# An adaptive-norm transformer block on one core: attention's channels in chunks of 112, score edges folded by 32, and an engine order written out

## The chip, the cores and the metric

The kernel runs on one core of one Trainium2 chip. The metric is the device time of one execution in microseconds, as the median of several runs. The core's engines work side by side, each through its own instructions in order: PE (matrix products), DVE (vector), ACT (activation functions), POOL (general), and SP, which here only issues DMAs. They wait for each other by semaphores.

## The reference

One sequence of 2048 positions with 448 channels goes through windowed attention and then a gated MLP that also mixes positions. Both halves are modulated by a vector c. Cut to what matters:

```python
mod = (silu(c) @ w_mod).reshape(1, 6, 1, 448)         # sa, ca, ga, sb, cb, gb
h = layernorm(x) * (1 + ca) + sa
q, k, v = heads(h @ wqkv)                             # 16 heads of 28
s = where(0 <= i - j < 256, q @ k.T * 28 ** -0.5, -1e9)
x = x + ga * (softmax(s) @ v) @ wo
h = layernorm(x) * (1 + cb) + sb
z = gelu(h @ w_in)                                    # 448 -> 1792
z1, z2 = z[..., :896], layernorm(z[..., 896:])
x = x + gb * ((z1 * (w_sp @ z2 + b_sp)) @ w_out)      # w_sp: 2048 x 2048
```

A query sees itself and the 255 positions before it. In blocks of 128 positions these lie in three key blocks: its own (lower triangle), the one before (all of it) and the one before that (upper triangle).

## The kernel before

Positions are 16 tiles of 128 in four blocks of 512. The 448 channels are the contraction of every projection and are held transposed (`hT`, channels on partitions) as four chunks: three of 128 and one of 64. The fourth chunk's other 64 rows are zeroed once in each weight (`t_p2`, `t_p3`, `t_p3v`, `t_p4`, lines 491 to 494), and products run over all 128 rows.

**Start.** `load3` (line 418) loads the columns of w_mod for the first modulation and then those of w_q and w_k together, each in three pieces over the queues of ACT and SP. The first four tiles of x come ahead of them in two pieces, one per queue. `t_mA` makes the modulation's columns, `mod_out` copies them to `modT`, and each chunk of the transposed, normalised x is scaled and shifted on its way out of PSUM into `hT` (lines 691 and 693). `t_wqk` (lines 595 and 596) copies the weights into `WQK`, where each head has 32 columns instead of 28. `warm` puts pairs of identity matmuls on PE as fillers; they have the lowest priority.

**Attention.** For each tile j, Q and K are projected into `qT` and `KT` (lines 725, 760 and 785; four heads in a group, 32 partitions a head) and V into `Vaug` (798). The scores are made with keys on partitions, in two halves of two head groups each (`half`; `qs` names the groups). In `fm` (line 901), four matmuls, one per head of a group, run on four row tiles of 32 partitions of the PE array, each into a PSUM bank of its own. In each bank of 512 columns stand: the middle key block for the first group (128 columns), and 192 columns for each group with the two triangles. Of both triangles a 64 x 64 corner is never seen, and two corners share 64 columns on different partitions: these products take 64 keys each, on column tiles of 64. The middle block of the second group has no room in the banks. It comes from one product of `KT` with `QBD`, a copy of Q in which each head's 32 partitions stand in columns of their own with zeros elsewhere, so that a single 512-column product gives four heads (line 910). `QBD` is filled by four DMAs a block (751, 777) into zeros that ACT wrote (`t_qz`, 528).

`unit` adds a product and the exp that empties it (line 862): per half one of 4 x 512 columns into `PW`, then one of 512 columns from the `QBD` product. `mask_all` (917) multiplies both triangles by 0/1 masks and spreads them out into `PT`, once per head group. The products with V (944) follow per head group; a column of ones in `Vaug` gives the row sums. Lines 958 and 960 divide. SP transposes the result by DMA into `hT`, `wo_g` projects it (969), 973 adds the residual, and statistics (603 to 609, with a power operation on POOL), normalisation (616, 622, 626), a DMA transpose and the second modulation (994) make the MLP's input.

**MLP.** Line 1066 makes z2 and 1087 z1, with two row tiles of 64 partitions; 1110 is the product with w_sp, and 1127 the last projection.

**What sets the order.** Each operation is added to a `Sched` with its dependences, a priority, PSUM banks or buffers that it takes (`Hold`, `Res`) and a duration on every engine that may run it: evictions from PSUM may run on ACT or DVE, some modulations on POOL too. `Sched.order` is a list planner. It keeps a clock per engine and takes, engine by engine, the operation that can start first, by priority among those; so it chooses engine, order and buffer. `PACE`, `PSTEP` and `LEAD` tie the next blocks' projections to the scores. `count` and `waits` turn the order into semaphore counts, and `emit` writes each engine's instructions.

Of the kernel before, what the change touches and what calls it, by code (L numbers as in the profile page):

```python
# [4 lines left out]
ACT = mybir.ActivationFunctionType  # L5
BF16 = mybir.dt.bfloat16
F32 = mybir.dt.float32

ENGS = ("pe", "act", "dve", "pool", "sp")
HOP = 0.12  # L10

BIAS = 0.0

NEXT = {"dve": 0.08, "act": 0.11, "pool": 0.045}

SHAPE = 0.1

TURN = 1.1
# [11 lines left out]
class Res:  # L30
# [6 lines left out]

    def best(self):
        found = None
        for o in self.options:  # L40
            at = 0.0
            for u in o:
                h = self.last[u]
                if h is None:
                    continue
                if not h.until or any(x.end is None for x in h.until):
                    at = None
                    break
                at = max([at] + [x.end for x in h.until])
            if at is not None and (found is None or at < found[0]):  # L50
                found = (at, o)
        return found
# [10 lines left out]
class Op:  # L63
    def __init__(self, n, ways, deps, prio, take, table, dma, lat, tail):
# [17 lines left out]
        self.shape = "full"  # L82

# [4 lines left out]
class Sched:  # L88
# [23 lines left out]
    def order(self):  # L112
        ready = {e: [] for e in ENGS}
        for op in self.ops:
            op.left = len(op.deps)
            for d in op.deps:
                d.users.append(op)
        free = {e: 0.0 for e in ENGS}
        table = [None]
        turned = [True]  # L120
        shape = ["full"]
        self.prog = {e: [] for e in ENGS}
        dma_at = [0.0]

        def enter(op):
            op.ready = max([0.0] + [d.start + d.ways["pe"][0] if d.eng == "pe" and "pe" in op.ways else d.end for d in op.deps])
            for e in op.ways:
                ready[e].append(op)

        for op in self.ops:  # L130
            if not op.left:
                enter(op)
        todo = len(self.ops)
        while todo:
            pick = None
            for e in ENGS:
                found = []
                for op in ready[e]:
                    if any(x.start is None for x in op.after):
                        continue  # L140
                    at = max(op.ready, free[e])
                    ok = True
                    for h in op.take:
                        b = h.res.best()
                        if b is None:
                            ok = False
                            break
                        at = max(at, b[0])
                    if ok:
                        found.append((at + (BIAS if e == "act" and len(op.ways) > 1 else 0.0), op))  # L150
                if not found:
                    continue
                first = max(free[e], min(a for a, _ in found))
                at, op = min(((a, o) for a, o in found if a <= first + 1e-9), key=lambda x: (x[1].prio, x[1].n))
                if pick is None or at < pick[0]:
                    pick = (at, e, op)
            assert pick is not None, "no op can go on"
            at, e, op = pick
            if e == "act" and len(op.ways) > 1:
                at -= BIAS  # L160
            for h in op.take:
                _, slot = h.res.best()
                h.slot = slot
                for u in slot:
                    old = h.res.last[u]
                    if old is not None:
                        op.deps.update(old.until)
                    h.res.last[u] = h
            op.deps.discard(op)
            dur, fns = op.ways[e]  # L170
            if e == "act" and op.table and op.table != table[0]:
                dur += 1.3
            if e == "pe" and op.shape != shape[0]:
                dur += SHAPE
                shape[0] = op.shape
            if e == "sp":
                if op.turn and not turned[0]:
                    dur += TURN
                turned[0] = op.turn
            op.eng, op.start = e, at  # L180
            free[e] = at + dur - NEXT.get(e, 0.0)
            if op.land is not None:
                op.end = max(at + 1.0, op.land)
                dma_at[0] = max(dma_at[0], op.end - 2.0)
            elif op.dma:
                dma_at[0] = max(dma_at[0], at + 1.0) + op.lat
                op.end = dma_at[0] + op.tail
            else:
                op.end = at + dur + HOP + op.lat
            if e == "act" and op.table:  # L190
                table[0] = op.table
            for x in op.ways:
                ready[x].remove(op)
            self.prog[e].append(op)
            todo -= 1
            for u in op.users:
                u.left -= 1
                if not u.left:
                    enter(u)
# [1010 lines left out]
```

## Time and profile before

| | |
|---|---|
| runs | 289.79, 290.8 and 291.15 us; median 290.8 |
| span of the profiled execution | 288.0 us, first to last instruction |
| PE | busy 274.4 us, 3432 matmuls |
| DVE | busy 170.3 us, 365 instructions |
| ACT | busy 131.8 us, 153 instructions |
| POOL | busy 123.4 us, 192 instructions |
| granted PE clock | 1.00 throughout |
| first projection on PE | 12.97 us (its weight load) |
| score exps (L862) | from 20.5 to 118.6 us, 69.4 + 6.1 us of ACT |
| products with w_sp (L1110) | from 167.1 us |

The profiled execution's own time is not listed apart from its span; against the median of the runs 2.8 us lie around the span. The span starts with the first instruction. A matmul's duration holds its way through the array, and matmuls overlap; so PE's busy time says when it had something in flight, and its rate is read from the distance between starts. Stages are best read from the chain of work that ended last and from busy time by stretches.

### The profile page before, as it was taken

Reading aid. Unit: us, or ns where it says so; the run is one execution under the profiler, and the core shown is the slowest. Engines: PE = TensorE matmul, PEld = TensorE weight load, DVE = VectorE, ACT = ScalarE, POOL = GpSimd, SP = SyncE. Lnnn points to the kernel's source line nnn. Section 1 sums busy time; section 2 is a strip of 40 time slices with the busy share of each in tenths; the row PEclk is TensorE's granted clock in tenths of the full one; section 3 lists DMA queues with packets and bytes.
Section 4 is the critical chain, followed back from the end, with each engine's and each line's share of the span. In section 5 each row is a group of like instructions: output and inputs, shape, how many; then the busy total and the mean of one; then the engine's idle time right before and its main releaser. Section 6 shows DMA issues by size and latency. Waiting matters only on the chain.

```text
span 288.0 us, 7864 instructions
## 1 busy us (share of the span) xinstructions
PE 274.4 (95%) x3432; PEld 151.4 (53%) x3432; DVE 170.3 (59%) x365; ACT 131.8 (46%) x153; POOL 123.4 (43%) x192
## 2 busy tenths in 40 slices
PE   6798889999999999999979999999999999999997
PEld 2595557567666765544445544444444444444443
DVE  7679996988889999879998101113211231123223
ACT  4487979999999988775656720000000000000000
POOL 8041690761470749898654113333133303330331
DMA  7845936244233685320199899940100010001001
GB/s 213 267 156 148 326 60 95 54 83 92 39 41 76 112 166 58 60 58 18 39 186 167 194 175 190 186 77 17 49 0 0 2 64 0 2 0 64 0 2 64
DMA packets 65349, 25.92 MB, mean 90 GB/s; under 512 B 56417, under 2 KB 64226, under 8 KB 65314
## 3 DMA queue, kind: packets, MB, share of 16 engines
q1 hardware_dynamic: 64496, 24.26, 40.3%
q10 hardware_dynamic: 818, 1.15, 1.3%
q8 instruction: 27, 0.44, 0.7%
q14 instruction: 8, 0.07, 0.1%
HBM read 9.01 MB, written 1.84 MB: 38 GB/s over the span
## 4 chain that ended last, share of the span: by engine, by line
PE 64%; DVE 20%; POOL 5%; DMA 5%; issue 2%; SPq 2%; ACT 1%; ACTq 1%; POOLq 0%
PE ps L1110 34%; PE ps L1127 7%; PE ps L1087 5%; DVE st_all L603 5%; DVE PT L917 5%; PE ps L785 4%; DMA wq_st<-in_A_wqkv_dram 3%; PE ps L944 2%; POOL rs_all L609 2%; PE ps L798 2%; PE ps L1066 2%; PE ps L901 2%; PE ps L725 2%; DVE xn L616 1%; DVE x_sb L973 1%
## 5 line engine op out<-in xcount | busy, mean ns | idle before, releaser
L862 ACT ACTIVATE PW<-ps 128x2048 bf16<-128x2048 f32 (+1 forms) x56 | 69.4, 1239 | 4.5 <-PE ps L901 3.2
L1117 POOL TENSOR_TENSOR z1T<-tmpg,z1T 128x512 bf16<-128x512 bf16 x28 | 32.3, 1153 | 89.9 <-DVE tmpg L1114 89.9
L1114 DVE TENSOR_TENSOR tmpg<-ps,bsp_bc 128x512 bf16<-128x512 f32 x28 | 19.4, 692 | 85.3 <-PE ps L1110 85.3
L1110 PE MATMUL ps<-wspB,z 128*128 128x512 bf16 x224 | 48.8, 379 | 0.0
L1110 PE MATMUL ps<-wspA,z 128*128 128x512 bf16 x224 | 48.7, 379 | 0.0
L917 DVE TENSOR_TENSOR PT<-PW,mask 128x1024 bf16<-128x1024 bf16 x56 | 38.7, 718 | 0.7 <-ACT PW L862 0.3
L1110 PEld LDWEIGHTS ps<-wspA,z 128*128 128x128 bf16 x224 | 21.9, 98 | 26.5 <-issue 0.4
L1110 PEld LDWEIGHTS ps<-wspB,z 128*128 128x128 bf16 x224 | 21.9, 98 | 26.4
L608 POOL TENSOR_SCALAR ve_all<-mv_all 128x1 f32<-128x1 f32 (+2 forms) x37 | 10.1, 274 | 47.3 <-DVE mv_all L606 46.5
L944 PE MATMUL ps<-Vaug,PT 128*128 128x32 bf16 x496 | 26.2, 177 | 2.8 <-issue 1.7
L944 PEld LDWEIGHTS ps<-Vaug,PT 128*128 128x128 bf16 x496 | 22.9, 96 | 7.0 <-issue 1.8
L609 POOL TENSOR_TENSOR rs_all<-ve_all,neghalf 128x1 f32<-128x1 f32 (+2 forms) x37 | 24.8, 672 | 2.0
L1066 PE MATMUL ps<-w_in,hT 64*128 64x448 bf16 x224 | 22.4, 349 | 2.1 <-POOL rs_all L609 1.7
L1087 PE MATMUL ps<-hT,w_in 64*128 64x512 bf16 x196 | 21.8, 376 | 0.0
L1127 PE MATMUL ps<-w_out_g,z1T 128*128 128x448 bf16 x112 | 21.8, 352 | 0.0
L944 PE MATMUL ps<-Vaug,PW 128*128 128x32 bf16 x224 | 21.7, 176 | 0.0
L944 PEld LDWEIGHTS ps<-Vaug,PW 128*128 128x128 bf16 x224 | 17.9, 96 | 2.9
L603 DVE BATCH_NORM_STATS2 st_all<-x_sb 128x6 f32<-128x448 bf16 x32 | 18.9, 609 | 0.4 <-DMA x_sb<-in_A_x_dram 0.3
L1073 ACT ACTIVATE z<-ps 128x896 bf16<-128x896 f32 x16 | 13.9, 915 | 11.2 <-PE ps L1066 11.2
L603 DVE BATCH_NORM_STATS2 st_all<-z 128x6 f32<-128x448 bf16 x32 | 18.1, 594 | 1.0 <-ACT z L1073 1.0
L622 POOL TENSOR_SCALAR xn<-x_sb,rs_all,ve_all 128x448 bf16<-128x448 bf16 x17 | 18.1, 1066 | 0.9
L1066 PEld LDWEIGHTS ps<-w_in,hT 64*128 64x128 bf16 x224 | 11.0, 94 | 12.5 <-ACT z1T L1095 2.1
(106 smaller groups left out, 370.1 us busy)
## 6 DMA issues: line engine op xcount, KB each, us to landing
out_dram<-fin SPq DMA_DIRECT2D x16, 112.0 KB, 1.7
x_sb<-in_A_x_dram SPq DMA_DIRECT2D x3, 448.0 KB, 4.4
wmod<-in_w_mod_dram SPq DMA_DIRECT2D x1, 1344.0 KB, 8.0
w_in<-in_B_w_in_dram SPq DMA_DIRECT2D x1, 1344.0 KB, 8.2
w_out_g<-in_B_w_out_dram SPq DMA_DIRECT2D x1, 784.0 KB, 5.4
QBD<-qT SPq DMA_DIRECT2D x12, 64.0 KB, 2.0
bsp_bc<-in_B_b_sp_dram SPq DMA_DIRECT2D x1, 512.0 KB, 5.4
wmod<-in_w_mod_dram SPq DMA_DIRECT2D x2, 224.0 KB, 6.2
```

What stands on the lines that cost most here:

```text
L603: st = [dve(0.62 if True else 0, lambda e, t=t, ci=ci, s=s: e.bn_stats(st_all[:, slot, t, ci, :], s()), deps(t), prio) for ci, s in enumer ...
L609: rs = pool(0.53 + 0.15 * len(tiles), lambda e: e.tensor_tensor(rs_all[:, slot, a:b], ve_all[:, slot, a:b], neghalf[:, 0:b - a], ALU.pow), ...
L622: "pool": (0.9, lambda e: e.tensor_scalar(to[:, h.slot[0], 0:D], x_sb[:, t, :], z, ve, ALU.mult, ALU.add))}, [nm], prio, [h])
L862: ex = act(xdur, lambda e, out_ap=out_ap, in_ap=in_ap: e.activation(out_ap(), in_ap(), ACT.Exp, scale=SCALE), [s], v - 8.0 + u, takes, tab ...
L917: return dve(0.70, lambda e: e.tensor_tensor(cols(hp.slot[0] * 2048 + 1024 * k, [[256, 4], [128, 2], [1, 128]]), cols(at_w() + 128 + 192 * ...
L944: fns.append(lambda e, hp=hp, hO=hO, hi=hi, bi=bi, kb=kb, hd=hd, nb=nb, a=at[hi][bi], p_of=p_of: e.matmul(ps[:, hO.slot[0], 32 * hd:32 * h ...
L1066: return lambda e, kc, p0, start, stop: e.matmul(ps[:, hs[t % 2].slot[hf], 0:D], lhsT=hT[p0:p0 + 64, kc, t * 128:(t + 1) * 128], rhs=w_in[ ...
L1087: return lambda e, kc, p0, start, stop: e.matmul(ps[:, hs[b // 2].slot[b % 2], :], lhsT=w_in[p0:p0 + 64, kc, ft * 128:(ft + 1) * 128], rhs ...
L1110: m = pe(16 * MMS, [lambda e, h=h, si=si, ft=ft, tb=tb: e.matmul(ps[:, h.slot[0], :], lhsT=z2[:, si, ft * 128:(ft + 1) * 128], rhs=(wspA i ...
L1114: a = dve(0.7, lambda e, h=h, ht=ht, tb=tb: e.tensor_tensor(tmpg[:, ht.slot[0], :], ps[:, h.slot[0], :], bsp_bc[:, tb * 512:(tb + 1) * 512 ...
L1117: u = pool(1.16, lambda e, ht=ht, ft=ft, tb=tb: e.tensor_tensor(z1T[tb][:, ft, :], tmpg[:, ht.slot[0], :], z1T[tb][:, ft, :], ALU.mult), [ ...
L1127: return [lambda e, ft=ft: e.matmul(ps[:, h.slot[0], 0:D], lhsT=z1T[t // 4][:, ft, (t % 4) * 128:(t % 4 + 1) * 128], rhs=w_out_g[:, ft, :] ...
```

## The change

- **Chunks.** Attention's 448 input channels become four chunks of 112 (`CP`). Rows 112 to 127 of an operand are neither loaded, zeroed nor read; the normalised x and attention's result are written with 16 columns of padding after every 112. The MLP keeps chunks of 128 and 64.
- **Loads.** The columns for the first modulation come in two pieces (two chunks each, one per queue), then w_k in two, then w_q in two, then the second piece of x. Weight copies go by chunk and part (`wqk`), and `t_mA` and the first tile's K projection run in two steps, the first needing only the first pieces. w_in is loaded in five pieces, each tied to the scores of a tile.
- **Projections as two operations.** `pe2` splits a projection's matmuls into two operations in the order, the second after the first.
- **Score edges.** The triangles are folded by 32: three products of 32 keys on column tiles of 32 stand in for the two of 64, and the two triangles of a group take 160 columns instead of 192. The 64 columns a bank that come free hold one half (64 queries) of the second group's middle block. The other halves, of both halves of the tile, come from two 256-column products with a smaller `QBD` into one bank, and one exp of 512 columns empties it for the whole tile. `PW` has three slots for whole tiles instead of five for halves.
- **Order.** `Sched.order` no longer plans: it reads `PLAN`, a string with every operation's engine, number and buffer options in order. `PACE`, `PSTEP` and `LEAD` change too. The `warm` pairs go from 18 to 16.

```diff
+PLAN = """
+a0 d20 t27 t24 t28 a2 t25 d21 a4 t26 a6 p45.0 a34 p46.1 s1 t22 p35.0 d84 p51.2 s3 p49.3 s5 p48.4 d82 s7 p42.5
+d85 d83 s8 t86 p44.1 t87 a36 s9 p40.0 s10 d89.0 t23 a76 d74 s11 p41 d88.1 a77 d75 p98.2 t30 a37 p55.3 d59 d58
+d80 d99 p56.4 d79 d78 a81 p101.5 p43.1 t31 a100 d102 t29 d90 a103 p113.0 d92 p125.1 p122.3 d91 t33 d93 t32
...
+p373.0 d349 a133 t159 p144.0 d351 a374.2 p350.0 p352 p145 s140 t166 p147.1 a146 t160 p148 d167.0 t162 p356
...
+        for at, word in enumerate(PLAN.split()):
+            n, *slots = map(int, word[1:].split("."))
+            op = self.ops[n]
+            for h, k in zip(op.take, slots):
+                h.slot = h.res.options[k]
...
+            op.eng = names[word[0]]
...
+        return [load(name + "ab"[i], ("act", "sp")[i], 0.4, lambda e, i=i: e.dma_start(
+            t[0:CP, 2 * i:2 * i + 2, cols], d[2 * CP * i:2 * CP * (i + 1), cols].rearrange("(c p) n -> p c n", p=CP)), (), prio, land) for i in range(2)]
...
+    t_wk = load3("d_wk", wq_st, A_wqkv, slice(D, 2 * D), -98.9, 8.3)
+    t_wq = load3("d_wq", wq_st, A_wqkv, slice(0, D), -98.8, 9.5)
+    t_x0.append(load_x0(1, "sp", -98.7, 10.3))
...
+    t_win_l = [load("d_win%d" % ch, "sp", 0.46, lambda e, ch=ch: e.dma_start(w_in[:, ch, :], B_w_in[ch * 128:(ch + 1) * 128, :]), (), -46.0 + 0.1 * ch)
+               for ch in range(3)]
...
+    def pe2(dur, fns, deps=(), prio=0.0, take=()):
...
+        first = pe(dur / 2, fns[:n], deps, prio, take)
+        then = pe(dur / 2, fns[n:], [first], prio - 0.01)
...
-    t_p2 = dve(1.2, lambda e: e.memset(wmod[64:128, 3, :], 0.0), prio=-98.0)
-    t_p3 = dve(0.43, lambda e: e.memset(wq_st[64:128, 3, :], 0.0), prio=-97.0)
...
-                for place in (((0, m, 128, 0, 128, 0, 0),), ((k, o, 128, 0, 64, 128, 0) for k in range(2)), ((k, n, 128, 64, 128, 256, 0) for k in range(2)),
-                              ((k, *e) for k in range(2) for e in ((n, 64, 0, 64, 192, 0), (o + 64, 64, 64, 128, 192, 64)))):
...
+                places = [(0, m, 128, 0, 128, at_m0, 0)]
+                places += [(k, o, 128, 0, 128, at_f[k], 0) for k in range(2)]
+                places += [(1, m, 128, here, here + 64, at_hm, 0)]
+                places += [(k, n, 128, 96, 128, at_f[k] + 128, 0) for k in range(2)]
+                places += [(k, n + 32 * g, 32, 32 * g, 96, at_f[k] + 32 * (g + 1), 32 * g) for k in range(2) for g in range(3)]
...
+                if half == 0:
...
+                    exC = unit(EPRI, 0.22, [lambda e, hC=hC, m=m, hh=hh, j=j, pair=pair: e.matmul(
+                        ps[:, hC.slot[0], 256 * hh:256 * hh + 256].rearrange("p (h q) -> p h q", h=4), lhsT=KT[:, 2 * hh + 1, m:m + 128],
+                        rhs=QBD[:, (j // 4) % 2, :, hh, pair:pair + 64], start=True, stop=True) for hh in range(2)],
+                         needC + [q_dma[j // 4]], 0.6, to_c, lambda hC=hC: ps[:, hC.slot[0], :].rearrange("p (a h q) -> p a h q", a=2, h=4), [], hC)
...
-                    mine = exs[:k + 1]
...
+                    mine = exs[:1] + (shared[1:] if k else [])
```

488 lines of the change are left out of this document (237 added, 251 removed).

## The prediction

> **What bounds the kernel now.** I read the page's busy table and slices first, then the chain of work that ended last, then busy time by stretches, then the groups of instructions, and the waits last.
>
> The stretches (window, its length, then busy time of PE, PEld, DVE, ACT and POOL with instruction counts) show four stages:
>
> ```profile
> 0.00:19.00 19.00, 15.15 (x176) 9.84 (x177) 13.36 (x43) 10.38 (x16) 7.23 (x22) 1.00 0.76 239
> 19.00:45.00 26.00, 22.72 (x476) 15.50 (x473) 23.63 (x54) 21.46 (x24) 16.15 (x25) 1.00 0.62 159
> 45.00:57.00 12.00, 10.95 (x293) 7.73 (x292) 9.90 (x19) 10.89 (x11) 5.73 (x5) 1.00 0.38 61
> 57.00:82.00 25.00, 24.93 (x601) 16.93 (x601) 22.48 (x45) 23.88 (x27) 11.38 (x21) 1.00 0.42 71
> 82.00:126.00 44.00, 42.87 (x965) 26.72 (x963) 39.37 (x85) 38.56 (x37) 28.03 (x48) 1.00 0.49 87
> 126.00:146.00 20.00, 17.86 (x172) 8.28 (x168) 20.00 (x48) 11.92 (x17) 16.10 (x31) 1.00 0.22 46
> ```
>
> Until 19 us the kernel loads and projects the first tiles. From 19 to 126 it does attention, where PE, DVE and ACT are all nearly full: 101.5, 95.4 and 94.8 us of 107. From 126 to 146 DVE has no free time. After 146 PE runs without a gap to the end, 142 us that the change leaves as they are, so whatever is won must be won before.
>
> The chain (start, length, what) says which engine ends last at each point:
>
> ```profile
> 2.36 7.77 DMA wq_st<-in_A_wqkv_dram
> 10.46 0.69 DVE WQK L596 x2
> 11.45 1.06 DVE hT L693 x3
> 13.16 0.89 PE ps L760 x16
> ...
> 33.12 2.88 DVE PT L917 x2
> ...
> 61.29 0.48 PE ps L901 x36
> 61.77 0.40 PE ps L944 x12
> 62.17 0.22 PE ps L910
> ...
> 145.89 2.83 PE ps L1066 x28
> ```
>
> The start hangs on the w_q/w_k load (to 10.13). From 57 to 82 the chain is all PE; from about 98 to 146 it alternates between DVE and POOL (masks, statistics, second normalisation). These groups price the edits:
>
> ```profile
> L862 ACT ACTIVATE PW<-ps 128x2048 bf16<-128x2048 f32 x28 | 52.7, 1881 | 3.7 <-PE ps L901 3.2
> L917 DVE TENSOR_TENSOR PT<-PW,mask 128x1024 bf16<-128x1024 bf16 x56 | 38.7, 718 | 0.7 <-ACT PW L862 0.3
> L862 ACT ACTIVATE PW<-ps 128x512 bf16<-128x512 f32 x28 | 16.7, 598 | 0.8
> L910 PE MATMUL ps<-QBD,KT 128*128 128x512 bf16 x28 | 10.7, 381 | 1.1 <-DMA QBD<-qT 1.1
> ```
>
> Each of 28 half tiles pays one exp of 2048 columns (1.88 us) and one of 512 (0.60 us).
>
> **The change, part by part.** The sum is made against the profiled execution, whose span is 288.0 us. The median of the runs is 290.8, so 2.8 us lie around the span, and I keep them.
>
> *Start.* One 224 KB piece of x moves behind the weights, and w_k comes before w_q. Before, 2.05 MB landed by 10.13 us, from 2.36 on: 264 GB/s. Without that piece the last weight lands about 0.23 MB / 264 GB/s = 0.9 us earlier, near 9.3. The weight copies on DVE are halves (eight instead of four, the 896-column one cost 0.39 us); three go to ACT. The four modT copies (0.07 us apart) become two. The first K projection needs the half-loaded w_k and the first two input chunks, so I place it at 10.6 instead of the first projection at 12.97: 2.4 us earlier. PE then has the second step of its order waiting for w_v, which was issued at 8.28 and took 3.1 us; that takes back up to 0.8 us. The late x piece (about 10.2, since the bytes are the same) still needs two statistics (1.2), their sums (0.3), POOL (1.0) and two normalisations (0.7) before its transposes near 13.4, and PE has ten halves of projections of about 0.45 us ahead of them, so it hides. Value: -1.6 us; ends -2.6 (all of the lead) and +0.5 (w_v or w_q late). The DVE memsets that go (1.18+0.43+0.24 us, and 0.24 later) ran mostly while DVE waited for x at 3.66; the zeroing of QBD, two ops of 1.05 us instead of four, ran while ACT waited for weights: both nothing; uncovered they would be worth at most 2 us, within that end.
>
> *Fewer exps.* Folding by 32 lets half of the fourth block share the main bank, so one 512-column exp serves a tile instead of two: 14 x 0.598 = 8.4 us less on ACT. The written order has eight more movable operations on ACT than before (45 against 37, two of them weight copies); six evictions of 0.60 us put 3.6 us back, leaving ACT 4.8 us lighter. DVE loses the same six at 0.62 to 0.69: 4.0 us lighter. The masks stay 56 of the same size. With all three engines near their limit, the stage shortens by about what both gain: -4.4 us. Ends: -8.4 (ACT alone set it) and 0 (the DVE and POOL chain after 98 does not move).
>
> *PE arithmetic.* Each 512-column product with QBD becomes one of 256 columns: a 512-column one holds the chain 0.22 us, sixteen of 128 columns 0.89, so 256 take about 0.11: 28 x 0.11 = -3.1. The folded scores rise from 36 to 48 matmuls a half. Inside one group of 36, four of 128 columns start 57 ns before the next four, of 64 columns 28 ns, the change of column tile takes 119 ns, eight in two column tiles 52. By those steps the new group takes about 0.56 instead of 0.48 us: 28 x 0.08 = +2.3. At the mean of 13.3 ns a matmul it would be +4.5. Net -0.8, ends -1.9 and +1.5; PE is the chain in about half of the stage, so -0.4.
>
> *Order and stalls.* In the stretches from 19 to 57 PE was free 3.28 + 1.05 = 4.3 us, much of it in single places: at 35.0 us it waited 1.8 us while two masks took 1.5 us each beside POOL's four gate products (4.53 us in one run, L592), and 1.1 us went in two waits for a QBD copy. The gate products now lie apart in POOL's order and the QBD copies move half the bytes. I take half of the 4.3: -2.0; ends -4 and +4, since an order written out can also stall where there was no stall.
>
> *At nothing.* Projections in two operations add no instruction, only places where others may slip in. The w_in load goes from three issues to five on SP (about 0.6 us each), tied to the scores of tiles 4 to 8; SP's later transposes wait 1.2 us more in all, and w_in is first read at 119.6. If that cover went, 1.2 us. Operands of 112 rows change no row's time. Eight filler pairs of identity matmuls ran at 109.5 to 117.5 (16 x 0.215 = 3.4 us) where DVE and POOL held the chain; that six such pairs now come late costs nothing unless PE is the chain there, 2.6 us at most. Three score slots of whole tiles replace five of half tiles: slightly more room.
>
> Sum: -1.6 - 4.4 - 0.4 - 2.0 = -8.4; 288.0 - 8.4 + 2.8 = 282.4 us.
>
> **The rivals.**
>
> *DVE and POOL keep the end (0.16).* From 98 on the chain is masks, statistics and POOL's power operation, of which the change removes none. Then the fewer exps give only -0.5 and the order -1.0; with -1.6 and -0.4 that is -3.5, 287.3 us. For it: DVE 20.00 of 20 us in 126 to 146. Against: six evictions leave DVE, and 2.76 us of DVE's time in 40 to 50 were free.
>
> *PE closes its gaps (0.16).* PE was free 3.28 + 1.05 + 0.07 + 1.13 + 2.14 = 7.7 us between 19 and 146, and filled 3.4 more. If the new order uses all 11.1: -11.1 - 1.6 - 0.4, 277.7 us. For it: three engines with 95 to 98 us of real work in 107. Against: in-order engines do not pack perfectly, and the new order itself places late fillers.
>
> *Slow start (0.08).* Rows of w_k and w_q are halved from 1792 to 896 bytes; such packets took 41 and 74 ns, so 896 x 41 / 16 = 2.30 against 2.07 us: 0.23 us more. If w_v also lands late and DVE's in-order weight copies hold up the hT evictions behind them, the start gives +0.5 instead of -1.6: 284.5 us. [...]
>
> *Slower (0.12).* The shared exp is a new wait: the second product of a tile's first half (L944) needs it, and ACT now runs it behind both 1.88 us exps. All later PE work queues behind that product. At 14 tiles, each us of PE wait costs 14 us; from 0.60 us a tile the 8.4 are gone, and at 0.8 us it ends at 282.4 + 11.2 = 293.6. For it: ACT order puts the shared exp last. Against: PE has projections and the second half's scores to run ahead of that product, and before its waits for masks were 1.6 us in all.
>
> **How the numbers follow.** Forecast 0.48, 282.4 (its own range 279.5 to 286); the rivals 0.16, 0.16, 0.08, 0.12. The range 276.5 to 288.8 leaves out the slower rival and the edges of two others. Half a per cent, 1.5 us, is about what a measurement can tell from no change. Faster: 0.48 + 0.16 + 0.08 + 0.13 = 0.85; same 0.06 (0.03 each of the first and the last rival); slower 0.09.
>
> **What would show it.** First projection on PE near 10.6 us; 14 exps of 512 columns; last score exp near 112 instead of 118.6; groups of 48 score matmuls in 0.56 us; no wait of L944's line on the shared exp; PE's gapless stretch beginning near 138 instead of 145.9. Wrong would be PE waits on L944 above 0.6 us a tile, DVE full to the same 146 us, or a first projection after 12 us.

## The result and the profile after

The changed kernel takes 289.11 us (median of 20 runs, 287.13 to 292.97) against 290.27 us for the kernel before on the same chip: a ratio of 0.9954, with a 95% interval from 0.9931 to 0.9976. (Medians here and below are over all runs; the ratios leave out the slow ones, and where the two differ the text goes by the ratios.) The forecast was 282.4 us, so of 8.4 us that were to be gained 1.2 came. The profiled execution took 289.01 us, with a span of 287.3 instead of 288.0. So 1.7 us lie around the span, here and (1.67 to 1.88) in every execution on record but one of e6 with 2.3, and not the 2.8 of the prediction, whose span of before belongs to an execution about 1.1 us quicker than the median beside it.

The stretches of the changed kernel, cut as before (window, its length, busy time of PE, PEld, DVE, ACT and POOL with instruction counts, granted PE clock, DMA share, GB/s):

```profile
0.00:19.00 19.00, 16.08 (x158) 10.48 (x159) 10.75 (x31) 9.04 (x15) 7.28 (x20) 1.00 0.92 239
19.00:45.00 26.00, 24.44 (x592) 17.10 (x590) 22.25 (x51) 21.98 (x26) 10.55 (x18) 1.00 0.28 72
45.00:57.00 12.00, 12.00 (x359) 8.86 (x357) 10.03 (x23) 10.97 (x11) 4.48 (x6) 1.00 0.74 84
57.00:82.00 25.00, 22.81 (x613) 15.64 (x612) 19.67 (x42) 19.85 (x20) 18.74 (x28) 0.93 0.67 139
82.00:126.00 44.00, 42.00 (x1144) 29.09 (x1125) 40.46 (x83) 35.53 (x32) 22.25 (x40) 1.00 0.51 78
126.00:146.00 20.00, 19.87 (x188) 9.27 (x188) 15.78 (x40) 12.28 (x20) 14.71 (x33) 1.00 0.28 57
```

The load did go: from 126 to 146 VectorE is busy 15.78 of 20 us (it was 20.00), and from 82 to 126 ScalarE 35.53 us (38.56). But in the stretch from 57 to 82, which had 0.07 us of PE's time free, 2.19 us are free, and the granted clock is 0.93. The groups say where ScalarE's relief went (busy time, mean ns, then idle time just before and what ended it):

```profile
L862 ACT ACTIVATE PW<-ps 128x2048 bf16<-128x2048 f32 x28 | 52.6, 1877 | 10.0 <-PE ps L906 9.4
L925 DVE TENSOR_TENSOR PT<-PW,mask 128x1024 bf16<-128x1024 bf16 x56 | 38.3, 709 | 2.3 <-ACT PW L862 2.2
L862 ACT ACTIVATE PW<-ps 128x512 bf16<-128x512 f32 x14 | 8.4, 600 | 2.5 <-PE ps L917 2.3
```

The 512-column exps are 14 of 600 ns, as forecast, 8.3 us less than before; ahead of the large exps ScalarE now waits 9.4 us for score products where it waited 3.2. It has become idle time. (Line numbers differ from kernel to kernel: L906 here is L901 before, L917 is L910, L925 is L917.)

What happens between 57 and 82 us is in the timeline of SP and of PE (start, length, what):

```profile
66.06 0.59 SPq L428 DMA_DIRECT2D w_in<-in_B_w_in_dram  x1
66.70 1.27 SPq L459 DMA_TRANSPOSE hT<-o_sb  x1
68.02 1.27 SPq L459 DMA_TRANSPOSE hT<-xn  x1
69.33 2.60 SPq L740 DMA_DIRECT2D QBD<-qT  x3
71.98 0.61 SPq L428 DMA_DIRECT2D w_in<-in_B_w_in_dram  x1
72.63 0.60 SPq L740 DMA_DIRECT2D QBD<-qT  x1
```

```profile
72.50 0.61 PE L906 MATMUL ps<-qT,KT 32*128 32x128 bf16 x48
73.04 1.07 PE L774 MATMUL ps<-hT,WQK 112*128 112x128 bf16 x16
76.06 0.61 PE L917 MATMUL ps<-QBD,KT 128*128 128x256 bf16 x2 [1.95 <-DMA QBD<-qT]
```

Tile 8's product with QBD needs four small copies on SP. The last qT that they read was out of PSUM at 68.33. The written order puts an MLP transpose (68.02) ahead of three of them and half a chunk of w_in (71.98) ahead of the fourth, which lands at 76.01. PE, in order, waits 1.95 us. The order on SP is not all of the lateness: this copy was 3.4 us under way, where the three before it took 1.9 to 2.7 us; why, the trace doesn't say. And PE does not come back at full speed, as three windows show:

```profile
72.67:76.08 3.41, 1.46 (x65) 1.23 (x55) 3.02 (x7) 1.88 (x1) 3.04 (x5) 1.00 0.56 128
76.08:79.50 3.42, 3.42 (x76) 2.21 (x77) 1.40 (x2) 1.15 (x3) 0.81 (x2) 0.50 0.47 92
79.50:82.91 3.41, 3.41 (x93) 2.08 (x90) 2.08 (x5) 2.95 (x3) 0.86 (x1) 1.00 0.37 66
```

Behind the wait the granted clock is 0.50 for 3.42 us, and products of 448 columns start 373 ns apart where elsewhere it is 189 ns: 1.7 us more are lost (half of 3.42), which busy time doesn't show.

Last, the chain of work near the end of the MLP's first part. Before, PE carried it from 145.89 on. Now it goes through SP, one transpose of w_sp after another:

```profile
141.59 1.18 SPq L459
142.83 1.25 SPq L459
...
159.57 1.95 SPq L459
161.57 1.30 SPq L459
...
186.44 3.68 DMA wspB<-in_B_w_sp_dram
190.16 69.24 PE ps L1123 x320
```

The first product with w_sp needs all 16 transposes of w_sp's first half. The last of them is issued at 161.57 and lands at 165.64; PE is done with z1 at 165.26 and the product starts at 165.78. Before, the last one landed at 165.10 and PE came to the product at 167.05 without a wait.

To see where PE's time goes I took the distance from each matmul's start to the next, less the distance at which such matmuls follow each other when nothing is late (216 ns for 512 columns, where each is recorded as 379 ns long, and 25 for 32; a score group as a whole). What is left over, with the filler products, by stage, in us; for the kernel called *both edits*, see the experiments:

| from : to | before | after | both edits |
|---|---|---|---|
| 0 : 18.5 | 8.92 | 9.15 | 9.76 |
| 18.5 : 57 | 7.18 | 5.40 | 5.71 |
| 57 : 98 | 2.04 | 5.33 | 2.71 |
| 98 : 126 | 5.69 | 5.62 | 5.41 |
| 126 : 168 | 2.78 | 0.89 | 0.31 |
| 168 : end | 3.08 | 3.71 | 3.48 |
| sum | 29.69 | 30.10 | 27.38 |
| useful PE work | 255.87 | 254.93 | 254.85 |

(The last row of stages moves by a microsecond with matmul records that are missing from a trace. With one-column products taken at 25 ns the second row is 6.4 before and 5.4 after; the three rows from 57 to 168 hardly move.) So the useful work fell by 0.94 us, the stalls did not fall in sum, and what was won before 57 us and after 126 was lost between 57 and 98.

### The profile page after: what moved, and what is told of

It reads as the page before. It is cut to its first block, busy times and chain, and to the rows that moved or that the text cites. A ratio compares the mean times of both kernels' runs of the same rounds, so it can differ in the third digit from the quotient of the medians.

```text
span 287.3 us, 8463 instructions
## 1 busy us (share of the span) xinstructions
PE 274.7 (96%) x3764; PEld 154.1 (54%) x3764; DVE 164.7 (57%) x353; ACT 124.4 (43%) x144; POOL 119.4 (42%) x192
## 4 chain that ended last, share of the span: by engine, by line
PE 65%; SPq 16%; ACT 6%; DVE 5%; DMA 4%; issue 2%; POOL 2%; POOLq 0%
PE ps L1123 25%; SPq L459 15%; PE ps L1140 7%; PE ps L953 5%; PE ps L906 5%; PE ps L774 4%; PE ps L714 4%; PE ps L794 3%; PE ps L547 3%; PE ps L979 2%; ACT PW L862 2%; DMA hT<-xn 1%; ACT PT L862 1%; PE ps L749 1%; DMA wspB<-in_B_w_sp_dram 1%
## 5 line engine op out<-in xcount | busy, mean ns | idle before, releaser
L862 ACT ACTIVATE PW<-ps 128x2048 bf16<-128x2048 f32 (+1 forms) x42 | 60.5, 1452 | 12.5 <-PE ps L906 9.4
L1127 DVE TENSOR_TENSOR tmpg<-ps,bsp_bc 128x512 bf16<-128x512 f32 x28 | 19.3, 692 | 80.3 <-PE ps L1123 52.9
L1123 PE MATMUL ps<-wspA,z 128*128 128x512 bf16 x224 | 49.3, 379 | 0.5 <-ACT z1T L1108 0.5
L1123 PE MATMUL ps<-wspB,z 128*128 128x512 bf16 x224 | 49.5, 379 | 0.0
L925 DVE TENSOR_TENSOR PT<-PW,mask 128x1024 bf16<-128x1024 bf16 x56 | 38.3, 709 | 2.3 <-ACT PW L862 2.2
L1123 PEld LDWEIGHTS ps<-wspA,z 128*128 128x128 bf16 x224 | 21.9, 98 | 27.2 <-issue 1.0
L1123 PEld LDWEIGHTS ps<-wspB,z 128*128 128x128 bf16 x224 | 21.8, 98 | 26.7 <-DMA wspB<-in_B_w_sp_dram 0.5
L953 PE MATMUL ps<-Vaug,PT 128*128 128x32 bf16 x496 | 25.5, 177 | 1.7 <-DVE PT L946 1.1
L590 POOL TENSOR_TENSOR rs_all<-ve_all,neghalf 128x1 f32<-128x1 f32 (+2 forms) x37 | 25.8, 716 | 1.4
L953 PEld LDWEIGHTS ps<-Vaug,PT 128*128 128x128 bf16 x496 | 22.8, 96 | 5.2 <-DVE PT L946 1.3
L953 PE MATMUL ps<-Vaug,PW 128*128 128x32 bf16 x224 | 20.9, 177 | 0.5 <-issue 0.5
L584 DVE BATCH_NORM_STATS2 st_all<-z 128x6 f32<-128x448 bf16 x32 | 18.4, 608 | 3.5 <-ACT z L1086 3.4
L953 PEld LDWEIGHTS ps<-Vaug,PW 128*128 128x128 bf16 x224 | 17.9, 97 | 3.6 <-issue 1.5
L1108 ACT ACTIVATE z1T<-ps 128x512 bf16<-128x512 f32 x28 | 14.6, 601 | 8.9 <-PE ps L1100 8.9
L906 PE MATMUL ps<-qT,KT 32*128 32x128 bf16 (+5 forms) x1344 | 17.5, 199 | 0.9 <-ACT PW L862 0.9
L906 PEld LDWEIGHTS ps<-qT,KT 32*128 32x128 bf16 (+1 forms) x1344 | 13.7, 91 | 8.3 <-ACT PW L862 5.3
```

Of the source, the lines that this page charges most:

```text
L584: st = [dve(0.62 if True else 0, lambda e, t=t, ci=ci, s=s: e.bn_stats(st_all[:, slot, t, ci, :], s()), deps(t), prio) for ci, s in enumer ...
L590: rs = pool(0.53 + 0.15 * len(tiles), lambda e: e.tensor_tensor(rs_all[:, slot, a:b], ve_all[:, slot, a:b], neghalf[:, 0:b - a], ALU.pow), ...
L862: ex = act(xdur, lambda e, out_ap=out_ap, in_ap=in_ap: e.activation(out_ap(), in_ap(), ACT.Exp, scale=SCALE), [s] + list(after), v - 8.0 + ...
L906: fm.append(lambda e, hm=hm, qi=qi, key=key, kn=kn, lo=lo, hi=hi, col=col, p0=p0, t=t, j=j: e.matmul(ps[p0:p0 + kn, hm.slot[t], col:col + ...
L925: return dve(0.70, lambda e: e.tensor_tensor(cols(hp.slot[0] * 2048 + 1024 * k, [[256, 4], [128, 2], [1, 128]]), cols(at_w() + pad + at_f[ ...
L953: fns.append(lambda e, hp=hp, hO=hO, hi=hi, bi=bi, kb=kb, hd=hd, nb=nb, a=at[hi][bi], p_of=p_of: e.matmul(ps[:, hO.slot[0], 32 * hd:32 * h ...
```

## The experiments

Two theories were on record. *Load theory*: attention is as long as ScalarE's and VectorE's load, the fold shortens it, and something gives that back. *Stall theory*: PE is the bound already, and its free time comes from single late operations. Later ones: *hand-over*, that a stall won before 140 us is lost again at w_sp's transposes; *start*; and *clock*.

| kernel | median us | ratio to before, 95% |
|---|---|---|
| after | 289.11 | 0.9954 [0.9931, 0.9976] |
| e1_planner | 293.64 | 1.0085 [1.0052, 1.0117] |
| e5_fold_alone | 294.85 | 1.0114 [1.0065, 1.0164] |
| e6_rest_alone | 292.98 | 1.0051 [1.0019, 1.0084] |
| e4_before_halfexp | 290.95 | 1.0006 [0.9983, 1.0029] |
| e2_exc_twice | 292.27 | 1.0018 [0.9991, 1.0045] |
| e3_qbd_ahead | 288.51 | 0.9893 [0.9849, 0.9937] |
| e7_wsp_early | 289.85 | 0.9935 [0.9903, 0.9967] |
| e8_qbd_wsp (both edits) | 286.75 | 0.9843 [0.9813, 0.9874] |
| e10_exc_twice_clean | 287.14 | 0.9873 [0.9834, 0.9913] |
| e9_start | 288.03 | 0.9868 [0.9825, 0.9911] |
| e11_fill_wait | 290.32 | 1.0001 [0.9969, 1.0034] |
| e12_fill_wsp | 287.77 | 0.9914 [0.9887, 0.9941] |

### The parts, each under the planner of before

The changed kernel's operations in the order that the planner of before makes:

```diff
     def order(self):
-        for at, word in enumerate(PLAN.split()):
-            n, *slots = map(int, word[1:].split("."))
...
+        while todo:
+            pick = None
+            for e in ENGS:
...
```

> All the changed operations, but ordered by the list planner of before instead of by the written order. Stall theory (PE's free time comes from single late operations, not from the load of ACT and DVE, so taking 8.4 us off ACT moves nothing by itself): 288 to 291 us, within 1% of before, with about as much PE time lost as in both kernels (30 us of filler and stalls). Load theory (the fold shortens attention by about 4 us and the written order gives that away again at one place): 285 to 286.5 us, 1.5 to 2% under before.

Before, with the fold and nothing else (shared exp, small QBD, three slots, its `PACE`, `PSTEP` and `LEAD`):

```diff
-    NPW = 5
+    NPW = 3
+    QP = (2, 0, 3, 1)
...
-    QBD, _, qbd_bytes = alloc("QBD", [128, 2, 2, 4, 512], BF16, at=wspA_off)
+    QBD, _, qbd_bytes = alloc("QBD", [128, 2, 4, 2, 256], BF16, at=wspA_off)
...
+                places += [(k, n + 32 * g, 32, 32 * g, 96, at_f[k] + 32 * (g + 1), 32 * g) for k in range(2) for g in range(3)]
```

> Before, with the folding by 32, the shared exp and the smaller QBD alone (and the pacing constants that go with fewer exps), under before's planner. Stall theory: only the PE arithmetic shows, 3.0 us less for the QBD products and 2.1 more for the scores, so 289 to 291 us. Load theory: 4 us less, 286 to 287 us.

All but the fold (chunks of 112, loads, split projections), the reverse of that diff in the first kernel:

```diff
-    NPW = 3
-    QP = (2, 0, 3, 1)
+    NPW = 5
+    QP = (0, 1, 2, 3)
...
-    QBD, _, qbd_bytes = alloc("QBD", [128, 2, 4, 2, 256], BF16, at=wspA_off)
+    QBD, _, qbd_bytes = alloc("QBD", [128, 2, 2, 4, 512], BF16, at=wspA_off)
```

> Before, with everything but the fold (chunks of 112, split loads, late second piece of x, projections as two operations), under before's planner. Stall theory: the earlier first projection is given back while the late piece of x is waited for, 289.5 to 291.5 us. Load theory, with the start worth what the prediction gave it: 288 to 289 us.

All three are slower than before, outside both theories' numbers: under that planner neither the fold nor the rest is a gain by itself, and together they are not either. Against the first of the three the written order is worth 1.0085 - 0.9954 = 1.3%. The planner's orders have the same kind of stall as the written one, on PE (us in total, times, longest). Of the first kernel's waits:

```profile
PE ps L947 <- DMA QBD<-qT: 3.3, 2, 2.0
```

and of the one without the fold:

```profile
PE ps L934 <- DMA QBD<-qT: 2.5, 1, 2.5
```

The kernel with the fold alone has no QBD wait over 0.6 us, but one of 2.6 us ahead of score products at 38.2 us. The late operation differs; a late operation there is in each.

### The load itself

The kernel before, with shorter exps and nothing else:

```diff
-                to_e = lambda at_w=at_w: PW[:, at_w() + 2048:at_w() + 2560]
+                to_e = lambda at_w=at_w: PW[:, at_w() + 2048:at_w() + 2304]
...
-                     need + [q_dma[j // 4]], 0.6, to_e, lambda hC=hC: ps[:, hC.slot[0], :], [], hC)
+                     need + [q_dma[j // 4]], 0.6, to_e, lambda hC=hC: ps[:, hC.slot[0], 0:256], [], hC)
```

> The kernel before in its own order, with the 512-column exps of the second four heads' middle block cut to 256 columns; what it leaves out: heads 2 and 3 of that block take the probabilities of heads 0 and 1. Nothing else changes, no wait and no order. ScalarE loses about half of 14 exps of 512 columns and of the ones beside them, at some 0.25 us each, 3.5 us or more. Load theory: attention shortens by 2 to 4 us, 286.5 to 288.5 us. Stall theory: 289 to 290.8 us, within 0.5 per cent of the kernel before.

```profile
L862 ACT ACTIVATE PW<-ps 128x2048 bf16<-128x2048 f32 x28 | 52.6, 1877 | 6.5 <-PE ps L901 6.4
L862 ACT ACTIVATE PW<-ps 128x256 bf16<-128x256 f32 x28 | 10.7, 384 | 0.8
```

ScalarE loses 16.7 - 10.7 = 6.0 us, its waits for score products grow from 3.2 to 6.4 us, and the time is that of before (1.0006). Load theory falls for ScalarE, and it falls on the kernel before, where the forecast was made.

The other direction, the changed kernel with every shared exp run twice:

```diff
+    spare, _, _ = alloc("spare", [128, 2, 512], BF16)
+    spares = []
...
+                    again = lambda e, j=j, hC=hC: e.activation(spare[:, j % 2, :], ps[:, hC.slot[0], :], ACT.Exp, scale=SCALE)
+                    exC.ways["act"] = (exC.ways["act"][0], [again, exC.ways["act"][1]])
```

> The changed kernel in its own order, with each of the 14 shared exps run twice on ScalarE, the second time into the place that counts, the first into a spare tile: 14 x 0.60 = 8.4 us more on ScalarE, as much as the fold took away. Load theory (ScalarE's and VectorE's load sets the length of attention): attention ends 4 us later, 292.5 to 294 us. Stall theory (TensorE is the bound already and its free time comes from single late operations; ScalarE now waits 9.4 us for score products): the load goes into ScalarE's waits, 289 to 290.5 us. What the second exp itself does on the path of one tile (its mask and its PV product wait 0.6 us longer) is inside the 1.4 us of this range.

8.4 us more on ScalarE cost 0.6% (1.0018 against 0.9954), some 1.9 us: by the ratio 290.8 us, between the two expectations and nearer to the Stall theory's; the median is nearer to the other one's. The profiled execution is one of the longest of its ten (295.16 us), so its rows don't say where the 1.9 us go. The same edit on a kernel without late copies (below) settles it.

### The late copy, and what was waiting behind it

The written order, with SP's copies for tile 8 ahead of the transpose and the load that have time:

```diff
-... s501 s372 s255 s253 s254 s19 s252 ...
+... s501 s255 s253 s254 s252 s372 s19 ...
```

> The changed kernel with one edit of SP's order: the four QBD copies of the third block go ahead of an MLP transpose and of a w_in piece that stood before and between them. Stall theory: the last copy lands some 2 to 3 us earlier, PE's wait of 2.1 us at 74 us goes, and with it the low granted clock in 72 to 79 us; 2.1 to 3.5 us less than the changed kernel, 285.6 to 287 us, ratio to before 0.984 to 0.989. Load theory: what is won there is lost at the next wait, less than 1 us from the changed kernel, ratio 0.992 to 0.997.

The wait at 74 us and its slow clock are gone. The last product with V ends at 117.6 us instead of 122.3: 4.7 us won. At the end 0.6% is left of that by the ratios, 1.8 us, just less than the Stall theory expected (the spans of the two profiles differ by 1.7). The rest is lost at w_sp's transposes, as the chain (start, length, what) says; L454 and L1118 are L459 and L1123 above:

```profile
157.14 1.30 SPq L454
158.44 0.04 issue
158.48 4.06 DMA wspA<-in_B_w_sp_dram
162.54 0.35 issue
162.89 7.24 PE ps L1118 x25
```

PE was done with z1 at 160.6 and waited 2.3 us for the last transpose of the first half. The transposes had moved with the end of attention (the first of the last 14 is issued at 136.9 instead of 141.6), but took 1.6 us longer in sum, the two longest 2.4 and 3.0 us where the changed kernel's took 2.0 each; why, the trace doesn't say. And again the granted clock falls behind the wait, to 0.50 for 3.41 us:

```profile
160.56:163.97 3.41, 1.13 (x7) 0.61 (x7) 0.00 (x0) 1.52 (x4) 0.00 (x0) 1.00 1.00 181
163.97:167.38 3.41, 3.41 (x10) 1.21 (x9) 0.00 (x0) 0.00 (x0) 0.00 (x0) 0.50 0.98 204
```

So I let the transposes come early. The fold made QBD and qT smaller, and the upper half of `wspA` shares its place with nothing now:

```diff
-        deps = [S_of[11], q_dma[2]] if si in (0, 1, 2, 3, 8, 9) else [all_S, list(q_dma.values())]
+        deps = [] if si > 7 else [S_of[11], q_dma[2]] if si < 2 else [all_S, list(q_dma.values())]
...
-... s320 s641 s818 s817 s669 ... s697 s725 ... s624 s596 ... s680 s652 s736 s708 s792 s819 s764 s830 s831 s824 ...
+... s320 s825 s641 s818 s817 s826 s669 ... s697 s827 s725 ... s624 s828 s829 s596 ... s680 s830 s831 s832 s819 s820 s652 s821 s736 s708 s822 s792 s823 s764 s824 ...
```

> The changed kernel with 14 of the 16 transposes of w_sp's first half put into SyncE's idle places between 88 and 136 us instead of after 141 us (the tile's upper half is free from the start, since the fold made QBD and qT smaller). SyncE's last one of them then starts near 145 us instead of 161.6. Hand-over theory (a stall won ahead of 140 us is given back at the first w_sp product, since w_sp's transposes keep SyncE from 141 to 188 us): alone it gives little, since that product started at 165.78 us with TensorE waiting 0.7 us for it at most: 288.0 to 289.3 us. If transposes from w_sp disturb QBD's and o's copies in attention it is slower, 290 to 292 us.

Alone this gives no difference that I would build on: 289.85 us on this chip and 0.9935, 0.2% below the changed kernel's ratio, with intervals that overlap. In its profile the last transpose of the first half is issued at 147.6 instead of 161.6, but the QBD copy is later than ever (PE waits 3.0 us, to 77.0, and the clock is 0.59 and 0.56 in the windows 78 to 80 and 80 to 82 us), so PE itself reaches that product at 167.4.

Both edits together:

```diff
-... s501 s372 s255 s253 s254 s19 s252 ... s320 s641 s818 s817 s669 ...
+... s501 s255 s253 s254 s252 s372 s19 ... s320 s825 s641 s818 s817 s826 s669 ...
```

> Both edits: the QBD copies of the third block ahead of the MLP's transpose and the w_in load on SyncE, and w_sp's first half early. The first edit alone gave 288.5 us and a new wait of 2.3 us for w_sp's first half at 160.2 us. Hand-over theory: this wait goes, the first w_sp product starts at 160.2 to 160.8 us instead of 162.9 (VectorE's last z is done at 160.0, so it is the next to decide), and the time is 286.0 to 286.9 us. Rival, VectorE's and ScalarE's work on z sets that point anyway: 288.0 to 288.8 us, with a wait for z in the place of the one for w_sp.

286.75 us, ratio 0.9843: the fastest of all these kernels, 1.1% below the changed one by the ratios. The two stretches that had the stalls:

```profile
57.00:82.00 25.00, 24.27 (x683) 17.01 (x684) 21.77 (x46) 21.89 (x21) 18.57 (x28) 1.00 0.80 140
...
126.00:146.00 20.00, 20.00 (x192) 9.35 (x190) 15.24 (x39) 12.28 (x19) 12.93 (x30) 1.00 0.84 146
```

No wait for w_sp and none above 0.1 us for QBD is left, and the clock is 1.00 in both. z1's matmuls run into the first w_sp product without a gap at 163.18 us. That is not the 160.2 to 160.8 that was expected, because this execution's start and attention were some 2.6 us later than in the profile with the first edit alone (last V product at 120.2); the time came out as expected all the same, which is in part luck. The wait that Hand-over theory named is gone, and with it the slow clock behind it: in the two profiles the first w_sp product starts 0.3 us later than with the first edit alone, and the span is 1.1 us shorter. The ratios alone don't show more than a sum: the wins are 0.2% and 0.6% apart and 1.1% together, and the intervals are 0.3 to 0.4% wide to each side.

Now the exps again, twice each, on this kernel:

```diff
+                    exC.ways["act"] = (exC.ways["act"][0], [again, exC.ways["act"][1]])
```

> The kernel with both SyncE edits and each of the 14 shared exps run twice, as before: 14 x 0.60 = 8.4 us more on ScalarE, where no late QBD copy and no late w_sp hides it. Load theory: 290.5 us or more, ratio over 0.997. Stall theory: TensorE stays the bound and ScalarE's 8 us of waits for score products take the most of it: 286.8 to 288.5 us, ratio 0.985 to 0.991.

```profile
L860 ACT ACTIVATE PW<-ps 128x512 bf16<-128x512 f32 x14 | 8.5, 608 | 0.0
L919 ACT ACTIVATE spare<-ps 128x512 bf16<-128x512 f32 x14 | 8.4, 601 | 0.5 <-PE ps L915 0.3
```

The same 8.4 us cost 0.3% (0.9873 against 0.9843, with overlapping intervals; 287.14 and 286.75 us), as Stall theory expects and far from what Load theory does. The last product with V ends at 120.0 us, where it ended at 120.2 without them.

### The start

The kernel with both edits, with the second piece of x earlier on SP, its statistics earlier on VectorE, and two filler pairs later on PE:

```diff
-a0 ... p46.1 s1 t22 p35.0 d84 p51.2 s3 p49.3 s5 p48.4 d82 s7 p42.5 d85 d83 s8 t86 p44.1 ... p41 d88.1 a77 d75 p98.2 ...
+a0 ... p46.1 s1 s8 t22 p35.0 d84 p51.2 s3 p49.3 s5 p48.4 d82 s7 d85 d83 d90 d92 d91 d93 t86 ... p41 p42.5 d88.1 a77 d75 p98.2 p44.1 ...
```

> The kernel with both SyncE edits (QBD copies ahead, w_sp early; 286.75 us, ratio 0.984) and a start with fewer holds: the second piece of x is the second transfer on SyncE instead of the fifth, its statistics stand ahead of the first piece's xn on VectorE, and two of the warming products go behind the modulation columns of the first chunk. Start theory (the change's earlier weights gained nothing since the first projection at 11.5 us is followed by a 0.6 us wait for that piece of x, and since warming products hold the modulation columns up to 8.5 us): modulation columns from about 7 us, first projection at 11.0 us, no wait for hT at 18 us, first scores at 19.5 us instead of 20.8, 285.3 to 286.3 us, ratio 0.979 to 0.983. Rival (the w_k landing at 8.3 to 8.9 us and its copies up to 11.5 us set the first projection, and 224 KB of x ahead of them makes them 0.6 us later): first projection at 11.8 us or later, 286.5 to 287.5 us.

The rival's mechanism holds, at twice its size. ScalarE's first copy of w_k in the kernel with both edits, and then in this one (start, length, what, idle time ahead and what ended it):

```profile
8.94 1.04 ACT L569 ACTIVATE WQK<-wq_st 112x448 bf16<-112x448 bf16 x2 [4.14 <-DMA wq_st<-in_A_wqkv_dram]
```

```profile
10.19 1.04 ACT L569 ACTIVATE WQK<-wq_st 112x448 bf16<-112x448 bf16 x2 [5.39 <-DMA wq_st<-in_A_wqkv_dram]
```

224 KB moved ahead make w_k 1.25 us late. The first projection goes from 11.96 to 13.15 us and the first scores from 20.76 to 21.21, and the time is 288.03 us (0.9868), no faster. In this order of the transfers too, what is moved ahead makes something else late.

### The slow clock behind a wait

The changed kernel, with four filler pairs in the place where PE waits for the copy, which stays late:

```diff
+    warm(4, [], 0.46)
     sc.order()
...
-... t451 p275 t452 p571.0 d556.0 ...
+... t451 p275 t452 p1185.0 p1186.0 p1187.0 p1188.0 p571.0 d556.0 ...
```

> The changed kernel with four more pairs of identity matmuls (8 x 0.215 = 1.7 us on TensorE) in the place where it waits 1.95 us for tile 8's QBD copy; the copy stays late and everything else as it is. In the changed kernel's profile the granted clock is 0.52 from 76 to 78 us and 0.63 from 78 to 80, 1.00 on both sides. Clock theory (the wait itself makes TensorE run at half clock for some 3.4 us behind it, 1.7 us lost): the clock stays 1.00 there, and attention ends 1.7 us earlier; of this at most 1.5 us show at the end, since w_sp's transposes are next: 287.5 to 288.5 us, ratio 0.989 to 0.993. Rival (the clock falls for another reason, or its loss is covered): clock still below 0.7 in that place, or 1.00 with 288.8 to 289.5 us.

```profile
74.00:76.00 2.00, 1.42 (x7) 0.46 (x5) 1.27 (x3) 0.75 (x1) 1.50 (x3) 1.00 0.33 107
76.00:78.00 2.00, 1.73 (x43) 1.27 (x44) 0.75 (x2) 1.08 (x2) 0.00 (x0) 1.00 0.63 124
78.00:80.00 2.00, 2.00 (x77) 1.49 (x66) 0.34 (x2) 1.52 (x1) 0.00 (x0) 1.00 0.40 81
```

The copy is as late (76.23 instead of 76.01), 0.9 us of the wait is left, and the clock stays 1.00 in this execution, as Clock theory expects. Over all executions that isn't shown: seven of its twelve have a mean granted clock of 0.998 or more, and nine of the changed kernel's twenty. The last product with V ends at 120.7 us, 1.6 earlier. But the time is 290.32 us (1.0001), slower than either theory said. Part of it is the hand-over again, in the waits:

```profile
PE ps L1118 <- DMA wspA<-in_B_w_sp_dram: 1.6, 1, 1.6
```

That takes back 1.1 of the 1.6 us: the product starts at 165.29 instead of 165.78. Why the time is 0.5% above the changed kernel's, the profile (span 287.2, of one of the quickest executions) doesn't say; the intervals overlap by a little.

The same filling where w_sp's first half is early:

```diff
+    warm(4, [], 0.46)
...
-... t451 p275 t452 p571.0 d556.0 ...
+... t451 p275 t452 p1185.0 p1186.0 p1187.0 p1188.0 p571.0 d556.0 ...
```

> The same four pairs of matmuls in the kernel with w_sp's first half early, where the copy is late too (a wait of 3.1 us at 73.8 us, clock 0.59 and 0.56 from 78 to 82 us) and where no transpose of w_sp holds back what is won: it took 289.85 us, and 286.75 with the copies ahead. Clock theory: half of that difference or more comes back without moving a copy: 287.6 to 288.6 us, ratio 0.986 to 0.990. Rival: within 0.2 per cent of 0.9935.

287.77 us, and 0.9914: by the median inside the clock theory's range, by the ratio just outside it and just outside the rival's too (0.2% better than without the fillers, with intervals that overlap). In its profile the clock is 1.00 in all windows from 70 to 84 us, and the wait that is left is 0.8 us. Here all executions bear it out: nine of ten have a mean granted clock of 0.998 or more, against two of eleven without the fillers. That the clock comes back is shown; what it is worth at the end is not settled by these runs.

## Why the prediction was wrong, step by step

**What failed first** is that attention did not get shorter. All four terms of the sum were to be won there or ahead of it, and its last product with V ends at 122.30 us against 121.97. What the span is shorter by was won behind it (times in us from the traces; the transposes are the last 14 of w_sp's first half):

| kernel | last V product ends | first of the transposes | last one landed | first w_sp product |
|---|---|---|---|---|
| before | 121.97 | 142.63 | 165.10 | 167.05 |
| after | 122.30 | 141.59 | 165.64 | 165.78 |
| e3_qbd_ahead | 117.56 | 136.93 | 162.54 | 162.89 |
| e11_fill_wait | 120.71 | 139.99 | 165.15 | 165.29 |

**Fewer exps, -4.4 us**, was the largest term, and its step "with all three engines near their limit, the stage shortens by about what both gain" is refuted for ScalarE. The load came off as forecast (14 exps of 600 ns), but e4 took 6.0 us off ScalarE for nothing (1.0006, from 0.9983 to 1.0029) and e10 put 8.4 us on for 0.3%. Of three engines that are 89 to 95% busy in a stretch, ScalarE was not the bound; it ran close behind PE, the fullest, because it waited for it (9.4 us ahead of the large exps, 3.2 before). The end of the bounds that the text called "0" was the true one. VectorE's share of the term (4.0 us lighter) was not tried by itself, and no run adds work to a busy PE; that PE is the bound is inferred.

**Order and stalls, -2.0 us**, with ends at -4 and +4. By the stages' table it is -0.5 us from 18.5 to 168: -1.8 before 57 us, about as forecast (the gate products lie apart, and the 1.8 us wait at 35 is one of 0.8 to 33.0; the link between the two was not tried), +3.3 from 57 to 98, where before only 0.07 us were free from 57 to 82, -1.9 from 126 to 168. "An order written out can also stall where there was no stall" was in the text, without a place and a price; the late QBD copy and the slow clock behind it are that stall, and e3 takes it away (last V product 4.7 us earlier). The place could have been read from the diff: SP's order for the third block's copies.

**The way to the end.** "After 146 PE runs without a gap to the end, so whatever is won must be won before" carried each win to the end in full. The changed kernel had no win in attention to carry, but e3 and e11 did, and not all of it arrived: of 4.7 us 2.9 at the first w_sp product and 1.7 at the end of the profile, of 1.6 us 0.5. The transposes follow the end of attention at the same distance (19.3 to 19.4 us in the last three rows), so a win moves them too. In these two executions the 14 took 25.6 and 25.2 us to the last landing, 24.1 in the changed kernel, and PE, which had been 1.95 us behind them before, had to wait. e8 shows the wait gone when they come early.

**Start, -1.6 us**, came out at about zero, and the step that failed is the last one, that the late piece of x hides. The first projection is at 11.52 us instead of 12.97 (10.6 forecast): the first fillers hold the modulation's columns until 8.5, and the weight copies end at 11.2. The last piece of w_q landed at 10.08 and not near 9.3. Then PE waits 0.4 us to 18.2 for the transposed second piece of x, which landed at 10.6 (10.2 forecast) and whose statistics began at 11.8 behind other work of VectorE, and the first scores come at 20.1 (18.4 before). e9, with x moved ahead, is no faster.

**PE arithmetic, -0.4 us**, is the term that was right and too small. By the distances between starts, the QBD products went from 6.03 to 3.04 us (-3.0; -3.1 forecast), and a score group from 0.48 to 0.54 us (0.56 forecast), in 28 groups +1.7 (+2.3 forecast). That is -1.3 for these two; all useful work fell by 0.94. That the span fell by about as much, 0.7 us, is chance: larger parts with both signs lie in it.

**At nothing.** The five w_in issues on SP were put at nothing with a cover of 1.2 us. One of them stands ahead of the fourth QBD copy and costs 0.65 us of the 1.95 us wait. The 112 rows show no cost in the spacing: projection matmuls of 128 columns follow at 56 ns before and after. The split projections were not tried by themselves; e6, which has them with the other loads, is 0.5% slower under the planner.

**The rivals.** "DVE and POOL keep the end" is nearest in number (287.3), and its mechanism did not hold: VectorE is not full from 126 to 146 any more (15.78 of 20 us), and the 1.7 us that PE waited for POOL's statistics ahead of 145.89 are gone. "Slower", by a wait for the shared exp on L944's line, did not come either: PE's waits of that line (L953 in the changed kernel) are 2.2 us in all, where 0.6 us a tile was written. "Slow start" had the direction: the start gained about nothing. No run here tried fewer and larger pieces.

Of what was to show it: the 14 exps and the score groups are as written. The last score exp ends at 119.8 us where 112 was written (119.2 before). PE is nearly without a gap earlier than written (from 126 instead of 138: 19.87 of 20 us to 146, and one wait of 0.5 us ahead of the first w_sp product).

## What to carry to other kernels

Before a win is carried to the end of the kernel, look for the next thing that the bound engine will wait for, a DMA queue above all, and ask whether it moves with the win and how much room is left; here it was 1.95 us before the change. When three engines are all near full, test which one is the bound by adding work to one of them: another can be busy only because it keeps pace. In an order written out, put the small copy that feeds the bound engine ahead of anything on its queue that has time: here the wait of 1.95 us for it had 1.7 us more behind it, lost to a clock of 0.50.

## What the runs showed of the hardware

Behind TensorE's wait of 1.95 us in the changed kernel and behind that of 2.3 us in e3, the granted clock was 0.50 for 3.41 to 3.42 us (both shown above), a loss of 1.7 us each. Behind the wait of 3.0 us in e7 it was 0.59 from 78 to 80 us and 0.56 from 80 to 82, which is 1.7 us again. It was 1.00 behind the two waits of 1.7 us in the kernel before (to 36.90 and 145.89), behind the 0.9 and 0.8 us that the fillers left in e11 and e12, and behind the 1.6 us in e11 ahead of the first w_sp product, at 165.29:

```profile
163.87:167.29 3.42, 2.00 (x10) 0.96 (x11) 0.00 (x0) 1.25 (x3) 0.00 (x0) 1.00 0.82 179
167.29:170.70 3.41, 3.41 (x18) 1.52 (x17) 0.00 (x0) 0.00 (x0) 0.00 (x0) 1.00 0.90 172
```

So few waits don't show what decides it.

Nor does one profile say what a wait costs in each execution. In the changed kernel's, the one stretch of 3.42 us at 0.50 makes a mean granted clock of 0.994 over 287.3 us. The record has that mean for each execution: the changed kernel's twenty lie near 1.000 (nine), 0.994 (seven) and 0.988 (four). Of the kernel before 71 of 83 executions beside the experiments lie at 0.994 or less, though its profile has 1.00 throughout. In which places the clock fell there, the record doesn't show.

Of 13 DMA transposes of w_sp in a row, 11 held SP's queue 1.33 to 1.35 us in the changed kernel, start to start, and two held it 2.0 us; the 13 took 18.7 us there and 20.3 in e3, where the two longest took 2.4 and 3.0. The last one took 4.1 us from issue to landing in both.
